# Row gathers ahead of a rarely taken branch, index products later, and row sums on another engine, in a kernel of attention and two mixtures of experts

## The chip, the cores and the metric

One core of one Trainium2 chip runs the whole kernel. The metric is the device time of one execution in microseconds (us). TensorE multiplies matrices, VectorE and ScalarE work on rows, GpSimd does so too and issues the gathers and scatters (indirect DMAs), and SP issues most plain loads. Each engine works through its own queue in order. In the profile they are PE (PEld for its weight loads), DVE, ACT, POOL and SP; a name with a q is the engine's sequencer or DMA queue.

## The reference

Attention over 8 heads (4 local, 4 strided), then two mixtures of experts (MoE), each row a token:

```python
x = attn(q, k, v)                                   # 1152 tokens x 512
logits = x @ w_gate + modality_bias[modality_id]    # MoE 1: 8 experts, each token goes to one
e_idx = argmax(logits, axis=1)
for e in range(8):
    out[e_idx == e] = gate * (relu(x[e_idx == e] @ w1[e]) @ w2[e])
for e in range(4):                                  # MoE 2: every token through all four
    y += p[:, e:e+1] * (relu(out @ w1b[e]) @ w2b[e])
```

## The kernel before

The work comes in four stretches. Attention and the router fill some 77 us. MoE 1 follows until about 205 us: the tokens of each expert are gathered by index into tiles of 128 rows. The fullest expert's first tile is done apart (`fill`). Two blocks of up to 464 tokens (`k` = 0 and 1, four tiles each, `NBT`) belong to the two fullest experts, a ninth tile (`S_ONE`) stands alone, and two small tiles (`NSM`, `sg`) hold up to 32 tokens of the experts with few. What doesn't fit goes through the body of `overflow` (L1515), which lies behind a chain of branches on the count `ntl_i` and isn't taken for these inputs. MoE 2 takes the rest of the time in units of hidden columns. A product in full float32 precision is made of three matmuls on high and low halves (`split`: ScalarE writes the high half, VectorE the low).

The schedule is written by hand. A loop over `n` runs layer 1 of block `k`, hidden chunk `fb` (`l1`, L1574), and two steps behind it layer 2 (`l2`, L1591). After each of them stands a `tick(k, fb, 0)` or `tick(k, fb, 1)` (L1761), which splits one more block of weights (`W.ahead`) and does what the table `todo` (L1741) has for that place. In this text (0,5,1) means the tick after layer 2 in step `fb` = 5 of block 0. The queues then follow the order in which the instructions are written.

Around the change:

- `slots_of` (L1056) computes from the router the list of token indices (`main.idx`) in small VectorE steps, given out by `steps`, and ends with matmuls that sum over tokens (L1152, L1153).
- `overflow` reads the count on every engine (L1516) and branches (L1521). Its body has a pool `op` with weight tiles `raw2_0..3`, rows `g` and `y`, and hidden tiles.
- `routed` (L1726) stands at (0,3,1): first `overflow`, then the pool `mp` on the memory that `op` gave back, with the split rows `xbh`, `xbl` of block 2 and its gathered tiles `gb`. Eight gathers on GpSimd fill them: four of rows (`xe`, L1622) and four of gates and other small values (`xx`, L738).
- `small_tiles` (L1632) loads the small tiles' weights in SP's queue and gathers `sg`; its matmuls are spread over the ticks from (0,6,0) on.
- `x_split(X[1], i, ...)` at (0,5,1) to (0,7,0) transposes a gathered tile into the PSUM bank `PA[0]` (L1171) and splits it (L1166, L1167) into `xbh` and `xbl`.
- `x2_load` (L1294) reads finished rows of MoE 1 back for MoE 2 from (1,2,0) on; `x2_prep` (L1321) transposes such a tile, takes four sums (L1311 to L1314) and four differences (L1319) on GpSimd, from (1,3,0) on.
- The tail (L1816 to L1844) weaves the ninth tile with the first unit of MoE 2; `PC.put(n)` splits `n` pieces of MoE 2's weights. A unit's fifth step ends with an addition on VectorE (L1448) that reads the PSUM bank which its sixth step goes on writing.

Block 2 in this text is the loop's second block, `k` = 1.

Of the kernel before, what the change touches and what calls it, by code (L numbers as in the profile page):

```python
# [20 lines left out]
P = 128  # L21
# [123 lines left out]
def fused_kernel(  # L145
# [1154 lines left out]
    def x2_sums(j, tt):  # L1300
# [10 lines left out]
        nc.gpsimd.tensor_tensor(t1, b12, b11, op=ALU.subtract)  # L1311
        nc.gpsimd.tensor_tensor(t2, b22, t1, op=ALU.subtract)
        nc.gpsimd.tensor_tensor(t4, b21, t2, op=ALU.subtract)
        nc.gpsimd.tensor_tensor(t3, b22, b12, op=ALU.subtract)  # L1314
        return b11, b21, b22

    def x2_split(h, l, src):
        nc.scalar.copy(h, src)
        nc.gpsimd.tensor_tensor(l, src, h.bitcast(F32), op=ALU.subtract)  # L1319

    def x2_prep(j):  # L1321

        cols = slice(HP * j, HP * (j + 1))
        t4 = ye0[:, :DM].rearrange("p (q c t) -> p q c t", q=4, c=2)
        b = x2_sums(j, [t4[:, i] for i in range(4)])
        gx.pop(j)
        for q, src in zip((QB11, QB21, QB22), b):
            x2_split(xh2[:, q, :, cols], xl2[:, q, :, cols], src)
        yield
        x2_split(xh2[:, QT1:, :, cols], xl2[:, QT1:, :, cols], t4)  # L1330

    def x2_late(j):
# [5 lines left out]
        b = x2_sums(j, tt)  # L1338
        gx.pop(j)
        for q, src in zip((QB11, QB21, QB22), b):  # L1340
            x2_split(*(x[:, :, cols] for x in XP[1][q]), src)
        yield
        for q, src in zip((QT1, QT2, QT3, QT4), tt):
            x2_split(*(x[:, :, cols] for x in XP[1][q]), src)
# [166 lines left out]
    with ExitStack() as mctx:  # L1511
# [3 lines left out]
        def overflow():  # L1515
# [3 lines left out]
            with tc.tile_pool(reuse_waits="tile", name="op", bufs=1) as op:  # L1519
                raws2 = [op.tile([P, 1024], F32, name=f"raw2_{i}") for i in range(KC)]  # L1520
# [111 lines left out]
        def small_tiles():  # L1632
# [14 lines left out]
            def fetch(n):  # L1647
                slot = [idxs[:, n : n + 1]]
                g = gathered(slot, mp, "sg", NSM)
                with_all(g, slot)  # L1650
                return g[0]

            for _ in ring:
                load()
            gs = [fetch(n) for n in range(NSM)]
# [58 lines left out]
        mp = None  # L1714
# [11 lines left out]
        def routed():  # L1726
            nonlocal small, mp
            overflow()
            mp = mctx.enter_context(tc.tile_pool(reuse_waits="tile", name="mp", bufs=1))
            X[1] = [mp.tile([P, KC, NBW], F32R, name=n) for n in ("xbh", "xbl")]  # L1730
            slots = [at(NBT + i) for i in range(NBT)]
            G[1] = gathered(slots, mp, "gb", NBT)
            with_all(G[1], slots)
            small = small_tiles()

        def fetch_one():
            G[2] = gathered([at(S_ONE)], gp, "g", None)
            with_all(G[2], [at(S_ONE)])
# [3 lines left out]
            (0, 0, 0): lambda: (steps(3), with_all(gA, [idx4[:, i : i + 1] for i in range(NBT)])),  # L1742
            (0, 1, 0): lambda: steps(2),
            (0, 2, 0): lambda: steps(2),
            (0, 2, 1): lambda: steps(1),
            (0, 3, 0): lambda: [0 for _ in rest],
            (0, 3, 1): routed,
            (0, 4, 0): copies,
            (0, 5, 0): lambda: next(small),
            (1, 2, 0): lambda: [x2_load(j) for j in range(CHT[0])],  # L1750
            (1, 2, 1): fetch_one,
# [3 lines left out]
        todo[1, 6, 1] = lambda: (split_one(), next(prep[3], None))  # L1755
        for j in range(CHT[0]):
            prep[j] = x2_prep(j)
            todo[1, 3 + j, 0] = lambda j=j: next(prep[j])
            todo.setdefault((1, 3 + j, 1), lambda j=j: next(prep[j], None))

        def tick(k, fb, n):  # L1761
# [6 lines left out]
            if (k, fb) >= (0, 6):  # L1768
                next(small, None)

        LAG = 2
        for n in range(2 * FC):
# [6 lines left out]
        bh, bl = (mp.tile([P, KC, NBW], F32, name=n).rearrange("p c n -> p (c n)") for n in ("xbh", "xbl"))  # L1779
# [52 lines left out]
        one_l2(0)  # L1832
        next(unit)
        next(unit)
        one_l2(1)
        PC.put(2)
        next(unit)
        next(unit)
# [209 lines left out]
```

## Time and profile before

| | us |
|---|---|
| median of 3 runs (lowest, highest) | 611.41 (610.82, 611.66) |
| the profiled execution | 608.61 |
| its span, first to last instruction | 606.8 |
| TensorE busy | 573.6 |
| VectorE busy | 355.3 |
| ScalarE busy | 284.7 |
| GpSimd busy | 242.3 |

The profile is one execution, so sums are made against its own time, 608.61. TensorE is busy in nearly all of the span. What it doesn't do is to be looked for in single waits, and in the stretches in which its granted clock is under 1.00 (1.00 is 2.4 GHz, the lower level is 1.2).

### The profile page before, as it was taken

The numbers are of one execution on the slowest core, as the hardware profiler recorded it, in microseconds if no ns is written. First come the engines' busy times: TensorE is split into PE (matmuls) and PEld (weight loads), VectorE is DVE, ScalarE is ACT, GpSimd is POOL, SyncE is SP. The second block draws the span as 40 slices with busy tenths as digits, with TensorE's granted clock in tenths as the row PEclk, the third lists the DMA queues.
The fourth block names the chain that finished last, engine by engine and source line by source line (L and its number), as shares of the span: only waits on it lengthen the run. The fifth ranks groups of instructions, "written<-read, shape, count | busy, mean of one in ns | idle before, by whom it ended". The sixth has DMA issues, their size and how long they took to land.

```text
span 606.8 us, 10107 instructions
## 1 busy us (share of the span) xinstructions
PE 573.6 (95%) x3746; PEld 483.1 (80%) x3746; DVE 355.3 (59%) x735; ACT 284.7 (47%) x617; POOL 242.3 (40%) x348
## 2 busy tenths in 40 slices
PE   8987987699799989999999999999999999999994
PEld 4555665577578878989889888989989899888893
DVE  6775877432224556686786776655575566557531
ACT  5754343333344645556656555444444444444410
POOL 6524332603566552455756674253222232222212
PEclk9999999889899989999999999999999999999998
DMA  8958423948923343524232232322223312111002
GB/s 261 314 127 278 154 88 109 321 181 273 326 75 105 120 177 110 187 73 136 70 129 80 86 123 71 138 88 105 87 70 98 111 71 70 69 70 70 0 9 79
DMA packets 33660, 77.55 MB, mean 128 GB/s; under 512 B 5856, under 2 KB 11882, under 8 KB 33477
## 3 DMA queue, kind: packets, MB, share of 16 engines
q1 hardware_dynamic: 28581, 65.66, 32.3%
q0 software_dynamic: 4736, 10.99, 5.4%
q8 instruction: 31, 0.51, 0.3%
q10 hardware_dynamic: 288, 0.19, 0.1%
q14 instruction: 24, 0.20, 0.1%
HBM read 73.46 MB, written 7.55 MB: 134 GB/s over the span
## 4 chain that ended last, share of the span: by engine, by line
PE 70%; issue 6%; DMA 3%; POOL 2%; DVE 1%; POOLq 0%; ACT 0%; DVEq 0%; ACTq 0%
PE ps_b L1436 10%; PE ps_b L1438 10%; PE ps_b L1437 10%; PE ps_b L1870 7%; PE ps_b L1869 7%; PE ps_b L1872 7%; PE ps_a L1870 4%; PE ps_a L1869 4%; PE ps_a L1872 4%; DMA g<-xc 1%; DMA sg<-xx,idxs 1%; PE ps_b L1600 1%; PE ps_b L1601 1%; PE ps_b L1602 1%; PE ps_a L1171 1%
## 5 line engine op out<-in xcount | busy, mean ns | idle before, releaser
L1358 DVE TENSOR_TENSOR wl<-stage,wh 128x512 fp32r<-128x512 f32 (+1 forms) x160 | 124.5, 780 | 58.7 <-ACT wh L1357 58.2
L1378 POOL TENSOR_TENSOR stage<-stage 128x256 f32<-128x256 f32 x32 | 24.0, 749 | 204.9 <-DVE wl L1358 204.9
L1357 ACT CAST wh<-stage 128x512 fp32r<-128x512 f32 (+1 forms) x160 | 102.8, 664 | 3.9 <-POOL mark L746 3.8
L1436 PE MATMUL ps_b<-x,wh 128*128 128x320 f32 x224 | 69.7, 311 | 0.2 <-DVE xl L1456 0.2
L1437 PE MATMUL ps_b<-x,wh 128*128 128x320 f32 x224 | 69.2, 309 | 0.0
L1438 PE MATMUL ps_b<-x,wl 128*128 128x320 f32 x224 | 69.0, 308 | 0.0
L1448 DVE TENSOR_TENSOR m2t<-ps_b,stage 128x320 f32<-128x320 f32 (+1 forms) x93 | 42.2, 453 | 41.0 <-PE ps_b L1438 39.9
L1436 PE MATMUL ps_b<-xh,wh 128*128 128x256 f32 x224 | 64.0, 286 | 2.2 <-DVE xbl L1448 2.2
L1438 PE MATMUL ps_b<-xh,wl 128*128 128x256 f32 x224 | 63.2, 282 | 0.0
L1437 PE MATMUL ps_b<-xl,wh 128*128 128x256 f32 x224 | 63.2, 282 | 0.0
L1436 PEld LDWEIGHTS ps_b<-xh,wh 128*128 128x128 f32 x224 | 42.5, 190 | 7.7 <-DVE xbl L1448 2.4
L1436 PEld LDWEIGHTS ps_b<-x,wh 128*128 128x128 f32 x224 | 42.0, 187 | 5.5 <-DVE xl L1456 0.4
L1437 PEld LDWEIGHTS ps_b<-xl,wh 128*128 128x128 f32 x224 | 42.5, 190 | 4.4
L1437 PEld LDWEIGHTS ps_b<-x,wh 128*128 128x128 f32 x224 | 42.1, 188 | 4.5
L1438 PEld LDWEIGHTS ps_b<-xh,wl 128*128 128x128 f32 x224 | 42.6, 190 | 0.0
L1438 PEld LDWEIGHTS ps_b<-x,wl 128*128 128x128 f32 x224 | 42.1, 188 | 0.0
L1451 ACT ACTIVATE hh2b<-m2t 128x256 fp32r<-128x256 f32 (+1 forms) x45 | 20.0, 444 | 43.3 <-DVE m2t L1448 40.8
L1167 DVE TENSOR_TENSOR wl<-stage,wh 128x1024 fp32r<-128x1024 f32 x24 | 30.6, 1280 | 15.5 <-ACT wh L1166 15.5
L1451 ACT ACTIVATE hh2a<-m2t 128x256 fp32r<-128x256 f32 (+1 forms) x42 | 18.7, 445 | 44.5 <-DVE m2t L1448 44.5
L1870 PE MATMUL ps_b<-wl,hh2b 128*128 128x512 f32 x90 | 35.7, 396 | 0.0
L1870 PE MATMUL ps_b<-wl,hh2a 128*128 128x512 f32 x90 | 35.5, 395 | 0.0
L1869 PE MATMUL ps_b<-wh,hh2a 128*128 128x512 f32 x90 | 35.5, 395 | 0.0
(398 smaller groups left out, 1411.0 us busy)
## 6 DMA issues: line engine op xcount, KB each, us to landing
stage<-in_w1b_dram SPq DMA_DIRECT2D x32, 512.0 KB
stage<-in_w2b_dram SPq DMA_DIRECT2D x32, 512.0 KB
stage<-in_w1a_dram SPq DMA_DIRECT2D x24, 512.0 KB
stage<-in_w2a_dram SPq DMA_DIRECT2D x24, 512.0 KB
g<-xc SPq DMA_DIRECT2D x5, 260.0 KB
vl<-in_vlo_dram SPq DMA_DIRECT2D x2, 520.0 KB
g<-xc POOLq DMA_DIRECT2D x4, 260.0 KB, 8.2
xe<-rw POOLq DMA_DIRECT2D x7, 128.0 KB, 5.4
```

What stands on the lines that cost most here:

```text
L1167: nc.vector.tensor_tensor(dst_l, src, dst_h.bitcast(F32), op=ALU.subtract)
L1357: return (lambda: nc.scalar.copy(h[:, s], src[:, s])), (lambda: nc.vector.tensor_tensor(l[:, s], src[:, s], h[:, s].bitcast(F32), op=ALU.s ...
L1358: lambda: nc.vector.tensor_tensor(l[:, s], src[:, s], h[:, s].bitcast(F32), op=ALU.subtract)
L1378: nc.gpsimd.tensor_tensor(a22, a22, a21, op=ALU.add)
L1436: nc.tensor.matmul(ph, wh[:, kc], xh, start=first and kc == 0, stop=False, skip_group_check=True)
L1437: nc.tensor.matmul(ph, wh[:, kc], xl, start=False, stop=False, skip_group_check=True)
L1438: nc.tensor.matmul(ph, wl[:, kc], xh, start=False, stop=kc == 1, skip_group_check=True)
L1448: nc.vector.tensor_tensor(t, a, b, op=ALU.add)
L1451: nc.scalar.activation(h, a, AF.Relu)
L1869: nc.tensor.matmul(po, hh, wh, start=(fb == 0 and fh == 1), stop=False, skip_group_check=part)
L1870: nc.tensor.matmul(po, hh, wl, start=False, stop=False, skip_group_check=part)
L1872: nc.tensor.matmul(po, hl, wh, start=False, stop=last, skip_group_check=part)
```

## The change

The gathers of block 2 and of the small tiles, and that of the ninth tile's rows, are written ahead of `overflow`. All their `xx` gathers follow right before it, at (0,5,0). The branch's body uses `raws[KC:]`, the weight buffers of block 1's second layer, for `raw2`. Block 2's tiles come from the pool `gp`, `sg` and the ninth tile from `mp`, which is opened ahead of the branch; only `xbh` and `xbl` lie on what `op` gives back (pool `mx`). The index products (the rest of `slots_of`) move from (0,3,0) to (0,4,0). One index step and one weight split are done ahead of the loop. The small tiles' first matmuls start a tick later. `x2_load` moves to (1,1,1), `x2_prep` to (1,4,0) to (1,5,1), one whole tile per tick, with its sums and differences on VectorE (`nc.vector`). One of the two pieces of `PC.put(2)` in the tail goes ahead by a few steps, one behind the next unit step.

```diff
--- before.py
+++ after.py
@@ -1297,7 +1297,7 @@
         eng.dma_start(out=g, in_=xc[P * j : P * (j + 1), :])
         gx[j] = g
 
-    def x2_sums(j, tt):
+    def x2_sums(j, tt, eng):
 
         g = gx[j]
         nc.gpsimd.tensor_copy(ext2[:, j], g[:, DM:])
@@ -1308,26 +1308,26 @@
         b = xr.rearrange("p (k c h t) -> p k c h t", k=2, c=2, h=2)
         b12, b21, b22, b11 = b[:, 0, :, 1], b[:, 1, :, 0], b[:, 1, :, 1], b[:, 0, :, 0]
         t1, t2, t3, t4 = tt
-        nc.gpsimd.tensor_tensor(t1, b12, b11, op=ALU.subtract)
-        nc.gpsimd.tensor_tensor(t2, b22, t1, op=ALU.subtract)
-        nc.gpsimd.tensor_tensor(t4, b21, t2, op=ALU.subtract)
-        nc.gpsimd.tensor_tensor(t3, b22, b12, op=ALU.subtract)
+        eng.tensor_tensor(t1, b12, b11, op=ALU.subtract)
+        eng.tensor_tensor(t2, b22, t1, op=ALU.subtract)
+        eng.tensor_tensor(t4, b21, t2, op=ALU.subtract)
+        eng.tensor_tensor(t3, b22, b12, op=ALU.subtract)
         return b11, b21, b22
 
-    def x2_split(h, l, src):
+    def x2_split(h, l, src, eng):
         nc.scalar.copy(h, src)
-        nc.gpsimd.tensor_tensor(l, src, h.bitcast(F32), op=ALU.subtract)
+        eng.tensor_tensor(l, src, h.bitcast(F32), op=ALU.subtract)
 
     def x2_prep(j):
 
         cols = slice(HP * j, HP * (j + 1))
         t4 = ye0[:, :DM].rearrange("p (q c t) -> p q c t", q=4, c=2)
-        b = x2_sums(j, [t4[:, i] for i in range(4)])
+        b = x2_sums(j, [t4[:, i] for i in range(4)], nc.vector)
         gx.pop(j)
         for q, src in zip((QB11, QB21, QB22), b):
-            x2_split(xh2[:, q, :, cols], xl2[:, q, :, cols], src)
-        yield
-        x2_split(xh2[:, QT1:, :, cols], xl2[:, QT1:, :, cols], t4)
+            x2_split(xh2[:, q, :, cols], xl2[:, q, :, cols], src, nc.vector)
+        yield
+        x2_split(xh2[:, QT1:, :, cols], xl2[:, QT1:, :, cols], t4, nc.vector)
 
     def x2_late(j):
 
@@ -1335,13 +1335,13 @@
         cols = slice(HP * i, HP * (i + 1))
         t4 = raws[6][:, :DM].rearrange("p (q c t) -> p q c t", q=4, c=2)
         tt = [t4[:, k] for k in range(4)]
-        b = x2_sums(j, tt)
+        b = x2_sums(j, tt, nc.gpsimd)
         gx.pop(j)
         for q, src in zip((QB11, QB21, QB22), b):
-            x2_split(*(x[:, :, cols] for x in XP[1][q]), src)
+            x2_split(*(x[:, :, cols] for x in XP[1][q]), src, nc.gpsimd)
         yield
         for q, src in zip((QT1, QT2, QT3, QT4), tt):
-            x2_split(*(x[:, :, cols] for x in XP[1][q]), src)
+            x2_split(*(x[:, :, cols] for x in XP[1][q]), src, nc.gpsimd)
 
     XP = {}
     RING2 = 8
@@ -1517,7 +1517,8 @@
                 ntl_i[0:1, 0:1], min_val=0, max_val=NSX, skip_runtime_bounds_check_because="bounded by the token count"
             )
             with tc.tile_pool(reuse_waits="tile", name="op", bufs=1) as op:
-                raws2 = [op.tile([P, 1024], F32, name=f"raw2_{i}") for i in range(KC)]
+                raws2 = raws[KC:]
+                assert W.ns >= 2 * KC
                 with ExitStack() as more:
                     more.enter_context(tc.If(ntl > S_OVF))
                     for t in range(S_OVF, NSX):
@@ -1644,15 +1645,9 @@
                     load_block(raw, todo.pop(0))
                     loaded.append(raw)
 
-            def fetch(n):
-                slot = [idxs[:, n : n + 1]]
-                g = gathered(slot, mp, "sg", NSM)
-                with_all(g, slot)
-                return g[0]
-
             for _ in ring:
                 load()
-            gs = [fetch(n) for n in range(NSM)]
+            gs = G["s"]
             yield
             used = 0
             bank = PA[1]
@@ -1711,7 +1706,8 @@
                 yield
 
         prep = {}
-        mp = None
+        mp = mctx.enter_context(tc.tile_pool(reuse_waits="tile", name="mp", bufs=1))
+        mx = None
 
         def copies():
             pr = PA[1][:, 64 : 64 + NSM]
@@ -1723,40 +1719,51 @@
             for _ in range(n):
                 next(rest)
 
-        def routed():
-            nonlocal small, mp
+        slotsB = []
+        slots_s = [idxs[:, n : n + 1] for n in range(NSM)]
+
+        def second_rows():
+            for _ in rest:
+                pass
+            slotsB.extend(at(NBT + i) for i in range(NBT))
+            G[1] = gathered(slotsB, gp, "g", None)
+
+        def small_rows():
+            copies()
+            G["s"] = gathered(slots_s, mp, "sg", NSM)
+            G[2] = gathered([at(S_ONE)], mp, "sone", 1)
+
+        def gates():
+            with_all(G[1], slotsB)
+            with_all(G["s"], slots_s)
+            with_all(G[2], [at(S_ONE)])
             overflow()
-            mp = mctx.enter_context(tc.tile_pool(reuse_waits="tile", name="mp", bufs=1))
-            X[1] = [mp.tile([P, KC, NBW], F32R, name=n) for n in ("xbh", "xbl")]
-            slots = [at(NBT + i) for i in range(NBT)]
-            G[1] = gathered(slots, mp, "gb", NBT)
-            with_all(G[1], slots)
+            mx = mctx.enter_context(tc.tile_pool(reuse_waits="tile", name="mx", bufs=1))
+            X[1] = [mx.tile([P, KC, NBW], F32R, name=n) for n in ("xbh", "xbl")]
+            return mx
+
+        def branch():
+            nonlocal small, mx
+            mx = gates()
             small = small_tiles()
-
-        def fetch_one():
-            G[2] = gathered([at(S_ONE)], gp, "g", None)
-            with_all(G[2], [at(S_ONE)])
+            next(small)
 
         small = None
         todo = {
-            (0, 0, 0): lambda: (steps(3), with_all(gA, [idx4[:, i : i + 1] for i in range(NBT)])),
+            (0, 0, 0): lambda: (steps(2), with_all(gA, [idx4[:, i : i + 1] for i in range(NBT)])),
             (0, 1, 0): lambda: steps(2),
-            (0, 2, 0): lambda: steps(2),
-            (0, 2, 1): lambda: steps(1),
-            (0, 3, 0): lambda: [0 for _ in rest],
-            (0, 3, 1): routed,
-            (0, 4, 0): copies,
-            (0, 5, 0): lambda: next(small),
-            (1, 2, 0): lambda: [x2_load(j) for j in range(CHT[0])],
-            (1, 2, 1): fetch_one,
+            (0, 2, 0): lambda: steps(3),
+            (0, 4, 0): second_rows,
+            (0, 4, 1): small_rows,
+            (0, 5, 0): branch,
+            (1, 1, 1): lambda: [x2_load(j) for j in range(CHT[0])],
         }
         for i in range(NBT):
             todo[0, 5 + (i + 1) // 2, (i + 1) % 2] = lambda i=i: x_split(X[1], i, G[1][i], PA[0])
-        todo[1, 6, 1] = lambda: (split_one(), next(prep[3], None))
+        todo[1, 6, 1] = split_one
         for j in range(CHT[0]):
             prep[j] = x2_prep(j)
-            todo[1, 3 + j, 0] = lambda j=j: next(prep[j])
-            todo.setdefault((1, 3 + j, 1), lambda j=j: next(prep[j], None))
+            todo[1, 3 + (j + 2) // 2, j % 2] = lambda j=j: [0 for _ in prep[j]]
 
         def tick(k, fb, n):
             early_ = (k, fb) < (0, 4)
@@ -1765,10 +1772,12 @@
             todo.get((k, fb, n), lambda: None)()
             if not early_:
                 W.ahead(RING, 1)
-            if (k, fb) >= (0, 6):
+            if (k, fb, n) >= (0, 6, 1):
                 next(small, None)
 
         LAG = 2
+        steps(1)
+        W.ahead(RING, 1)
         for n in range(2 * FC):
             k, fb = divmod(n, FC)
             l1(k, fb)
@@ -1776,7 +1785,7 @@
             if n >= LAG:
                 l2(*divmod(n - LAG, FC))
                 tick(k, fb, 1)
-        bh, bl = (mp.tile([P, KC, NBW], F32, name=n).rearrange("p c n -> p (c n)") for n in ("xbh", "xbl"))
+        bh, bl = (mx.tile([P, KC, NBW], F32, name=n).rearrange("p c n -> p (c n)") for n in ("xbh", "xbl"))
         first = {k: bl[:, 256 * i : 256 * (i + 1)] for i, k in enumerate("tabd")}
         sh = bh[:, :FF]
         parts = [hidden_parts() for _ in range(2)]
@@ -1830,11 +1839,12 @@
         one_htr(1)
         next(unit)
         one_l2(0)
+        PC.put(1)
         next(unit)
         next(unit)
         one_l2(1)
-        PC.put(2)
         next(unit)
+        PC.put(1)
         next(unit)
         one_l2(2)
         next(unit)
```

## Rows read from the trace of the kernel before

**Rows 1.** Waits of TensorE: line, releaser, us in all, times, longest

```profile
PE ps_a L1171 <- DMA sg<-xe,idxs: 4.9, 1, 4.9
...
PE ps_a L1171 <- DMA g<-xc: 3.6, 1, 3.6
...
PE ps_b L1436 <- DVE xbl L1448: 2.2, 1, 2.2
...
PE ps_a L1153 <- DVE bos L1147: 1.9, 1, 1.9
...
PE ps_b L1601 <- DVE wl L1167: 1.8, 1, 1.8
...
PE ps_b L1581 <- PEq L1521: 1.4, 1, 1.4
```

**Rows 2.** Stretches: us, busy PE, PEld, DVE, ACT, POOL, then PEclk, DMA, GB/s

```profile
75.00:100.00 25.00, 20.03 (x99) 15.08 (x98) 19.70 (x57) 9.56 (x13) 4.97 (x5) 1.00 0.30 98
...
119.30:124.80 5.50, 5.49 (x16) 4.27 (x16) 0.00 (x0) 0.59 (x1) 0.00 (x0) 0.51 0.59 225
...
162.50:166.00 3.50, 3.46 (x12) 3.03 (x13) 0.02 (x1) 2.28 (x6) 1.67 (x5) 0.56 0.98 393
...
215.40:220.40 5.00, 4.97 (x21) 4.36 (x22) 2.47 (x6) 2.52 (x6) 1.73 (x4) 0.66 0.16 61
...
166.00:194.00 28.00, 28.00 (x191) 22.37 (x191) 10.45 (x10) 13.70 (x28) 20.99 (x34) 1.00 0.25 81
...
221.00:600.00 379.00, 376.90 (x2206) 338.61 (x2205) 237.66 (x405) 184.01 (x407) 145.45 (x199) 1.00 0.26 91
```

**Rows 3.** L1516, L1521: xcount, ns min/median/max, first to last start us

```profile
L1516 POOLq TENSOR_LOAD <-ntl_i x1: 485/485/485, 80.4 to 80.4; - x1
...
L1521 POOLq EVENT_SEMAPHORE  x4: 17/43/43, 86.5 to 87.1; - x4
...
L1521 POOLq INC_SWDGE_SEM  x1: 796/796/796, 87.2 to 87.2; - x1
...
L1521 SPq EVENT_SEMAPHORE  x9: 17/17/17, 101.0 to 101.6; - x9
```

**Rows 4.** Timeline of GpSimd: start us, us, line, operation [idle <- releaser]

```profile
84.08 0.94 POOL L738 DMA_INDIRECT g<-xx,idx  x1 [0.30 <-issue]
...
101.92 0.94 POOL L1622 DMA_INDIRECT gb<-xe,idx  x1 [16.90 <-SPq L1521]
...
118.07 0.12 POOL L746 MEMSET mark<- 128x1 f32 x1
```

**Rows 5.** Timeline of SP, its loads around the branch

```profile
96.57 0.33 SPq L197 DMA_DIRECT2D stage<-in_w1a_dram  x1
...
107.25 5.09 SPq L197 DMA_DIRECT2D stage<-in_w1a_dram  x5
```

**Rows 6.** Tile gb, its eight gathers, issue to landing

```profile
DMA to landing us min/median/max: 2.8/6.0/7.8
```

**Rows 7.** Timeline of TensorE: transposes and the layer behind

```profile
119.31 1.11 PE L1171 MATMUL ps_a<-mk,sg 128*128 128x128 f32 x4 [4.89 <-DMA sg<-xe,idxs]
...
120.08 0.77 PE L1600 MATMUL ps_b<-wh,hh 128*128 128x512 f32 x1
...
171.19 0.60 PE L1171 MATMUL ps_a<-mk,g 128*128 128x128 f32 x4
```

**Rows 8.** Timeline of VectorE: a relu's low half, a tile's low half

```profile
102.73 0.64 DVE L1589 SCALAR_TENSOR_TENSOR hl<-ps_b,hh 128x464 fp32r<-128x464 f32 x1 [3.79 <-ACT hh L1588]
...
112.10 0.69 DVE L1167 TENSOR_TENSOR xbl<-ps_a,xbh 128x512 fp32r<-128x512 f32 x1 [1.08 <-ACT xbh L1166]
```

**Rows 9.** Timeline of GpSimd: the loads for MoE 2

```profile
155.94 2.25 POOL L1297 DMA_DIRECT2D g<-xc  x4 [3.34 <-DMA xc<-g,dest]
```

**Rows 10.** Timeline of VectorE: weight pieces, then the addition

```profile
212.35 2.69 DVE L1358 TENSOR_TENSOR wl<-stage,wh 128x768 fp32r<-128x768 f32 x3 [0.32 <-ACT wh L1357]
...
214.97 0.41 DVE L1448 TENSOR_TENSOR xbl<-ps_b,xbl 128x256 f32<-128x256 f32 x1
```

## The prediction

> **What bounds the kernel now.** I read the waits of TensorE first, because the chain that ends last runs through it. Only six waits over 1.3 us lie between 85 and 216 us [rows 1]. Then the table by stretch: from 221 us on, TensorE is busy 376.9 of 379 us at a granted clock of 1.00 [rows 2]. So the second mixture of experts (MoE 2) is a solid block, and what the stages before it win or lose arrives at the end one to one. The same table shows a second price of some waits: after the waits of 4.9, 3.6 and 2.2 us the granted clock was 0.51, 0.56 and 0.66 for 5.5, 3.5 and 5.0 us, so TensorE ran at the lower level (1.2 GHz) for part of each; after those of 1.4 to 1.9 us it stayed 1.00. Length times missing clock gives 2.7, 1.5 and 1.7 us.
>
> The profiled execution took 608.6 us (span 606.8), 2.8 us less than the median of 611.4. I sum against 608.6 and carry the difference of 2.8 over.
>
> **Parts that cost nothing or are covered.** One index step and one weight split move ahead of the loop. VectorE and ScalarE have only that to do before the first relu, and the third block's split then comes one layer-1 step (2.6 us) earlier, so the 1.8 us wait at L1601 goes. The index products move from (0,3,0) to (0,4,0), by when the counts (L1147) are done: the 1.9 us wait goes. The two gathers of the ninth tile (sone) join GpSimd's early burst and leave its queue at 158 us. Neither 1.8 nor 1.9 reaches the end by itself, since what follows is tied to GpSimd, below.
>
> **The branch: where the front gain goes.** Before, the gathers stood behind the branch. GpSimd itself had passed it: four events at 86.5 to 87.1 and one of 0.8 us at 87.2 [rows 3]. But the first gather waited 16.9 us, until 101.9, for SP's events at 101.0 to 101.6 [rows 3, 4], because its tile lies on memory that the branch's body uses. SP's events came 4.4 us after its last load was issued (96.57) [rows 5]; GpSimd's came 2.4 us after its last gather was issued (84.08) [rows 4]. I read both the same way: an engine reports the branch passed only when everything that it had issued before has landed, and whoever reuses the body's memory waits for that report.
>
> The change takes the gathers out of that wait, but puts fourteen of them (four rows of block 2, two small, one ninth, then seven of `xx`) ahead of the branch on GpSimd. The memory that is now laid over the body's g, y and he is `xbh`, first written by ScalarE in `x_split` at (0,5,1). So ScalarE waits for GpSimd's report, T:
> - The index is there when layer 1 of (0,4) is done. VectorE took up its low half at 102.73 [rows 8]; less 1.8 + 1.9 + 1.4 of waits and about 0.5 of products that lay ahead of it, that is 97.1. Add 0.6 (the low half), 0.2 (the index copy) and 0.3 (issue): the first gather starts at 98.2.
> - The fourteenth starts 13 paces later. One gather is 0.94 + 0.30 = 1.24 in a quiet stretch; the twelve of before took 101.92 to 118.07, 1.35 each [rows 4]. I take 1.3: 16.9.
> - It lands 2.8 to 7.8 us after issue [rows 6]; I take the middle, 5.3, since SP's loads are in flight. The report adds 0.9 (as 87.2 to 88.0).
> - T = 98.2 + 16.9 + 5.3 + 0.9 = 121.3; ends 118.0 (1.24, 2.8) and 124.4 (1.35, 7.8).
>
> Behind ScalarE's waiting instruction stand the next weight split and the relu of (0,6). TensorE, having split the first tile at about 107 and done layer 1 of (0,6), needs bank PA[0] for the second `x_split` at about 110 and waits there. After T come ScalarE 0.59 (its one copy of a tile, 128x512, in the stretch from 119.3 [rows 2]), VectorE 0.69 [rows 8], some 0.2 of handing over, and 0.77 for four transposes at the low clock (119.31 to 120.08) [rows 7]: layer 2 of (0,4) starts at T + 2.2, and 0.4 for the small tile's transposes is still owed. Before, it started at 120.08 with those done [rows 7]. The balance is T + 2.6 - 120.1 = T - 117.5 = **+3.8 us**, ends +0.5 and +6.9. The waits of 4.9, 1.9 and 1.8 are gone and one of some 12 stands for them; the low clock after it I take as before. The small tile's own gather, issued by 105, is no longer late. The branch's 1.4 on TensorE moves to (0,5,0) and hides under that wait; SP passes when its last load has landed, around 107, as it started the small weights at 107.25 before [rows 5].
>
> **Loading for MoE 2: -5.1 us.** The loads `g<-xc` were issued at 155.94, after 3.34 us for the last scatter's landing [rows 9], and TensorE waited 3.6 us for the first. Issuing them at (1,1,1) doesn't change that: they wait for the same scatter, except that the small tile's scatter now stands behind them. It must then wait for them to land, and GpSimd with it, but nobody needs that row soon. What helps is that the first transposes move from after layer 1 of (1,3) to after that of (1,4). The second tile's transposes stood there at 171.19 [rows 7]; less 162.5, where the first began, and less 1.5 for the low clock, that is some 7 us later. So 7 against 3.6: the wait and its low clock go, 3.6 + 1.5 = 5.1. If landing is late again, the clock's part may stay: 3.6 at the least.
>
> The sums now run on VectorE: per tile seven operations of 128x128 and one of 128x512. The trace has no such operation on VectorE. By its 128x512 split (0.69 [rows 8]) a quarter is 0.17 at least, and 0.41 (its 128x256 addition, [rows 10]) at most; I take 0.3, so 2.8 us a tile, 11 in all. VectorE was busy 10.5 of 28 us there [rows 2] and two steps lie between a relu and its use, so I cost it at nothing; at 0.41 it would be some 14, and about 1 us might show.
>
> **The hand-over to MoE 2: -3.0 us.** The 2.2 us wait at L1436 is for VectorE's addition at 214.97, which stood behind three weight pieces begun at 212.35 [rows 10]; two of them came from `PC.put(2)` right before that unit step. With one put moved ahead and one behind, I expect the pieces done by about 213.5 and the addition at once behind: a wait of some 0.9 is left, since the next product writes the bank that the addition reads. That is 1.3, and 1.7 of low clock, as waits under 2 us left the clock at 1.00. Ends: 0 (the pieces' load lands no earlier) and 3.9.
>
> **Sum.** 608.6 + 3.8 - 5.1 - 3.0 = 604.3 profiled, 607.1 as a median. All ends together: -8.5 and +3.3, so 602.9 to 614.7.
>
> **Rivals.**
> *The branch doesn't hold ScalarE.* If GpSimd's delay were only the jump, its report would come early: it read the branch's value at 80.4, while its gathers ran on until 85 [rows 3, 4], so its sequencer runs ahead. With the small index at about 101 and ten issues of 0.3 it is through at 104; 80.4 to 88.0 is 7.6 more: T = 111.6, -5.9 instead of +3.8: 597.4. With no wait on memory at all, 1.8 + 1.9 + 4.9 + 2.7 = 11.3 come off: 592.0. Against it: the 16.9 us wait, and the two reports that follow landings. The Trainium skill ("Runtime: NRT & Kernel Launch", Instruction fetch mechanics) says that a taken branch whose target isn't in the fetched window stalls for a fetch of it. By that rule the gaps after the branch would be fetches and the first of these two times would follow; the trace has such gaps but, as they differ between the engines and end with landings, doesn't bear it out alone. Chance 0.12 together.
>
> *The loads stay late.* If the burst and the small weights crowd the transfers so that `g<-xc` lands 3 us later against the work, or the put order wins nothing, some 3 of the 8.1 are lost: 610 to 611, within 0.2%. Chance 0.14.
>
> *Slower: GpSimd reports so late that the wait outgrows the rest.* The break-even is T = 117.5 + 8.1 = 125.6. SP's five loads, issued over 5.09 us from 107.25 [rows 5], fall just ahead of the last gathers. If those then need 12 us instead of at most 7.8, at 1.35 apiece, T = 98.2 + 17.5 + 12 + 0.9 = 128.6 and the time is 611.4 + 11.1 - 8.1 = 614.4. For it: landing already reached 7.8 under such load; against: those loads should be nearly through by 115. Chance 0.09.
>
> **How the numbers follow.** Forecast 0.65, rivals 0.12, 0.14, 0.09. The range of 602 to 613 takes in nearly all of the forecast, the second rival and the mild end of the third; it leaves out the first and the bad ends, under 2 in 10. About 0.2% (1.2 us) is what a measurement can tell from no change. Faster by more: 0.59 of the forecast, the first rival, and a little of the second, 0.73. Within: 0.15. Slower: the third and the forecast's worst end, 0.12.
>
> **What would show it.** In the changed profile: waits at L1601, L1153 and for `sg` gone; gathers on GpSimd from about 98 without a break; its branch events near 121; TensorE waiting some 12 us around 110 to 122 at L1171 for `gb`'s successor, with ScalarE's `xbh` behind GpSimd; no wait for `g<-xc`; under 1.5 us at L1436, the clock at 1.00 behind it; MoE 2 as long as before. It is wrong if `xbh` follows its transposes at once (much faster), or if the events come after 125 (no gain).

## The result and the profile after

| | time, us | ratio to before |
|---|---|---|
| before | 611.6 median (608.9 to 615.3) | |
| changed | 606.0 median (602.5 to 610.2) | 0.991, 95% interval 0.989 to 0.993 |
| profiled execution of the changed kernel | 607.0, span 605.3 | |

The change gains 5.6 us by the medians; 607.1 was predicted. The two profiled executions differ by 1.6 us only: single executions of either kernel scatter by some 3 us to both sides, and the one of before was 3 us under its median. So stretches of the two traces show what moved, and the medians what it is worth.

The waits of TensorE over 1.3 us between 90 and 225 us (tile, line, who released it, total, times, longest) answer to [rows 1]. Six waits have become three, and one is longer than all of the others together:

```profile
PE ps_a L1171 <- DVE xbl L1167: 11.6, 1, 11.6
PE ps_b L1601 <- PEq L1522: 2.5, 1, 2.5
PE ps_b L1436 <- DVE xbl L1448: 1.9, 1, 1.9
```

The waits for `sg`, `g<-xc`, `bos` and `wl` are gone. The chain that ended last in 95 to 130 us (start, us, what) tells where the 11.6 us come from, and the branch's line gives each engine's branch events (count, shortest/median/longest in ns, first and last start):

```profile
115.39 6.70 DMA sone<-xx,idx
...
122.48 0.59 ACT xbh L1166
...
123.09 0.70 DVE xbl L1167
...
123.84 1.12 PE ps_a L1171 x4
```

```profile
L1522 SPq EVENT_SEMAPHORE  x9: 2/17/704, 107.5 to 109.4; - x9
L1522 POOLq EVENT_SEMAPHORE  x4: 17/43/9302, 111.5 to 121.0; - x4
L1522 PEldq COMPARE_BRANCH  x1: 4652/4652/4652, 99.9 to 99.9; - x1
...
L1522 ACTq COMPARE_BRANCH  x1: 50/50/50, 102.8 to 102.8; - x1
L1522 DVEq COMPARE_BRANCH  x1: 72/72/72, 103.5 to 103.5; - x1
...
L1522 ACTq EVENT_SEMAPHORE  x1: 17/17/17, 108.1 to 108.1; - x1
L1522 POOLq COMPARE_BRANCH  x1: 53/53/53, 111.0 to 111.0; - x1
L1522 POOLq INC_SWDGE_SEM  x1: 1076/1076/1076, 121.1 to 121.1; - x1
```

GpSimd reaches the branch at 111.0, but one of its four events lasts 9.3 us, until the last of its fourteen gathers has landed. That one was issued at 115.39, the last packet of GpSimd's queue ended at 120.30 by the trace's transfer records, and the event at 120.88; the 6.70 us of the chain have the rest of the report (to 122.1) in them. ScalarE's first `xbh` follows at once, then VectorE, then TensorE. Layer 2 of (0,4) starts at 124.61; before, it was 120.08 [rows 7]. On GpSimd's timeline (start, us, operation, idle before it and who ended it) the gathers run from 97.74 without a break, where before the first came at 101.92 [rows 4]:

```profile
97.74 0.95 POOL L1623 DMA_INDIRECT g<-xe,idx  x1 [12.46 <-DVE cum L1157]
...
115.39 0.94 POOL L738 DMA_INDIRECT sone<-xx,idx  x1 [0.30 <-issue]
```

The table by stretch (as [rows 2]: us, busy PE, PEld, DVE, ACT, POOL, clock, DMA share, GB/s) has the low clock behind the long wait as before, 0.50 over 5.5 us against 0.51, but 1.00 where it had been 0.56 and 0.66. From 221 us on it shows the same solid block as before:

```profile
123.80:129.30 5.50, 5.46 (x15) 4.32 (x16) 3.60 (x4) 2.20 (x4) 0.00 (x0) 0.50 0.35 118
...
162.50:166.00 3.50, 3.50 (x28) 2.28 (x27) 1.87 (x2) 1.77 (x3) 1.19 (x3) 1.00 1.00 296
...
214.50:220.00 5.50, 5.18 (x31) 4.63 (x32) 5.09 (x9) 3.64 (x7) 1.62 (x3) 1.00 0.31 102
221.00:600.00 379.00, 375.27 (x2193) 336.53 (x2191) 236.94 (x403) 182.22 (x404) 144.96 (x199) 1.00 0.26 90
```

### The profile page after: what moved, and what is told of

The parts are those of the page before. It is cut to its first block, busy times and chain, and to the rows that moved or that the text cites. A ratio compares the mean times of both kernels' runs of the same rounds, so it can differ in the third digit from the quotient of the medians.

```text
span 605.3 us, 10092 instructions
## 1 busy us (share of the span) xinstructions
PE 573.7 (95%) x3746; PEld 482.7 (80%) x3746; DVE 363.7 (60%) x767; ACT 284.7 (47%) x617; POOL 221.6 (37%) x316
## 4 chain that ended last, share of the span: by engine, by line
PE 76%; DMA 2%; DVE 1%; issue 1%; ACT 0%; POOL 0%; POOLq 0%; ACTq 0%
PE ps_b L1436 10%; PE ps_b L1437 10%; PE ps_b L1438 10%; PE ps_b L1880 7%; PE ps_b L1879 7%; PE ps_b L1882 7%; PE ps_a L1880 4%; PE ps_a L1879 4%; PE ps_a L1882 4%; PE ps_b L1601 2%; PE ps_b L1602 2%; PE ps_b L1603 2%; PE ps_b L1582 1%; PE ps_b L1584 1%; PE ps_b L1583 1%; PE ps_a L1171 1%
## 5 line engine op out<-in xcount | busy, mean ns | idle before, releaser
L1436 PE MATMUL ps_b<-x,wh 128*128 128x320 f32 x224 | 69.7, 311 | 0.2 <-DVE xl L1456 0.2
L1448 DVE TENSOR_TENSOR m2t<-ps_b,stage 128x320 f32<-128x320 f32 (+1 forms) x93 | 42.2, 454 | 40.4 <-PE ps_b L1438 37.8
L1436 PE MATMUL ps_b<-xh,wh 128*128 128x256 f32 x224 | 63.9, 285 | 1.9 <-DVE xbl L1448 1.9
L1436 PEld LDWEIGHTS ps_b<-xh,wh 128*128 128x128 f32 x224 | 42.2, 188 | 8.1 <-DVE xbl L1448 2.1
L1436 PEld LDWEIGHTS ps_b<-x,wh 128*128 128x128 f32 x224 | 42.0, 187 | 5.4 <-DVE xl L1456 0.4
L1167 DVE TENSOR_TENSOR wl<-stage,wh 128x1024 fp32r<-128x1024 f32 x24 | 29.2, 1222 | 14.6 <-ACT wh L1166 8.5
```

What stands on the lines that cost most here:

```text
L1167: nc.vector.tensor_tensor(dst_l, src, dst_h.bitcast(F32), op=ALU.subtract)
L1436: nc.tensor.matmul(ph, wh[:, kc], xh, start=first and kc == 0, stop=False, skip_group_check=True)
L1448: nc.vector.tensor_tensor(t, a, b, op=ALU.add)
```

## Experiments

Each was timed against the kernel before on the same chip; "gain" is against the changed kernel's 606.0. The kernel before had medians from 610.1 to 611.6 in these rounds, so where two medians of different rounds differ by little, the ratios decide.

| kernel | median, us | ratio to before, 95% interval |
|---|---|---|
| front_alone | 616.3 | 1.009 (1.006 to 1.012) |
| no_x2 | 613.6 | 1.004 (1.001 to 1.006) |
| before_put | 608.7 | 0.998 (0.996 to 1.001) |
| no_put | 607.3 | 0.994 (0.991 to 0.998) |
| sums_on_gpsimd | 607.0 | 0.993 (0.990 to 0.996) |
| before_x2 | 604.5 | 0.991 (0.989 to 0.994) |
| own_rows | 599.6 | 0.981 (0.977 to 0.985) |
| gates_behind | 597.1 | 0.977 (0.972 to 0.982) |
| early_branch | 593.4 | 0.974 (0.970 to 0.978) |
| own_rows_four_behind | 592.8 | 0.972 (0.969 to 0.974) |
| own_rows_gates_behind | 592.3 | 0.967 (0.964 to 0.971) |
| no_branch | 590.9 | 0.969 (0.964 to 0.974) |

### The parts, one by one

**front_alone**: x2 and `PC.put` as before, only the changes around the branch kept.

```diff
-        b = x2_sums(j, [t4[:, i] for i in range(4)], nc.vector)
+        b = x2_sums(j, [t4[:, i] for i in range(4)], nc.gpsimd)
...
-            (1, 1, 1): lambda: [x2_load(j) for j in range(CHT[0])],
+            (1, 2, 0): lambda: [x2_load(j) for j in range(CHT[0])],
...
-            todo[1, 3 + (j + 2) // 2, j % 2] = lambda j=j: [0 for _ in prep[j]]
+            todo[1, 3 + j, 0] = lambda j=j: next(prep[j])
+            todo.setdefault((1, 3 + j, 1), lambda j=j: next(prep[j], None))
...
         one_l2(0)
-        PC.put(1)
         next(unit)
         next(unit)
         one_l2(1)
+        PC.put(2)
         next(unit)
-        PC.put(1)
```

> The changed kernel with the loading for MoE 2 put back (loads at (1,2,0), sums on GpSimd at the old steps) and both of the PC.put back in one place: only the changes around the branch are left. By the prediction's sum the front alone costs +3.8 (ends +0.5 and +6.9) against the kernel before: 612.1 to 618.5 beside a median of 611.6, middle 615.4, with waits of some 12 us at L1171, 3.6 us for the loads g<-xc and 2.2 us at L1436. Rival (the medians of the two kernels differ by 5.6 us although the profiled pair differs by 1.6, so the front was worth nothing or a gain): 609 to 612.

It is 5.2 us slower than the kernel before (611.1 on that chip), by the ratio 5.4 with an interval of 3.7 to 7.1. The predicted +3.8 and its ends hold; the rival, that the front is worth nothing, falls. The waits are those expected, with 4.7 us for `g<-xc` in place of 3.6 and 13.7 at L1171, since GpSimd's report ended 2.0 us later in this execution (124.1) than in the changed kernel's:

```profile
PE ps_a L1171 <- DVE xbl L1167: 13.7, 1, 13.7
PE ps_a L1171 <- DMA g<-xc: 4.7, 1, 4.7
PE ps_b L1601 <- PEq L1522: 2.6, 1, 2.6
PE ps_b L1436 <- DVE xbl L1448: 2.2, 1, 2.2
```

**no_x2**: the changed kernel with the x2 part of that diff alone.

> The changed kernel with the loading for MoE 2 as before: the loads g<-xc at (1,2,0), the row sums and splits on GpSimd at the old steps. With the changed kernel's front alone the wait for these loads was 4.7 us and the granted clock behind it 0.94 over 28 us (1.7 us), so the later loads should cost 4.7 + 1.7 = 6.4 us here: 612.4. By the prediction's own term (5.1): 611.1. Rival (alone in the kernel before the move was worth 5 to 6 us, but here the small tile's scatter stands behind the loads): 607 to 609.

613.6: the loading for MoE 2 is worth 7.6 us in the changed kernel. The wait for `g<-xc` is 4.7 us, until 166.75, and the clock then stays low: 0.50 until 170 and 0.76 over the next 4 us, which loses 1.6 and 1.0 us. That makes 7.3 by the profile, where I had put 3.6 + 1.5:

```profile
166.75 1.12 PE L1171 MATMUL ps_a<-mk,g 128*128 128x128 f32 x4 [4.74 <-DMA g<-xc]
```

```profile
166.00:170.00 4.00, 3.25 (x21) 0.50 0.24 96
170.00:174.00 4.00, 4.00 (x16) 0.76 0.28 99
```

**before_x2**: the same part alone in the kernel before.

> The kernel before with the loading for MoE 2 alone changed: the loads g<-xc at (1,1,1), the row sums and splits on VectorE, at the changed kernel's steps. By the prediction -5.1 us (at the least -3.6), so 606 to 607.5 beside 611.3; the wait of 3.6 us for g<-xc and the low clock behind it go, and VectorE's sums show nowhere on TensorE. Rival (the gain needs the front's other order, or the sums delay the relu): 609 to 612.

604.5 beside 610.8: 6.3 us by the medians, 5.3 by the ratio (3.5 to 7.0). Here the wait that goes is the one of 3.6 us [rows 1], so the term of 5.1 is confirmed at its own place; in the changed kernel it grew because the wait it takes away had grown. The earlier place of the loads isn't what helps: GpSimd still issues them only after 3.46 us of waiting for the last scatter, where it was 3.34 [rows 9], as the prediction had it:

```profile
160.93 2.25 POOL L1297 DMA_DIRECT2D g<-xc  x4 [3.46 <-DMA xc<-g,dest]
```

**sums_on_gpsimd**: loads and steps as changed, `nc.vector` back to `nc.gpsimd` in `x2_prep`.

> The changed kernel with the loads and steps as changed, but the row sums and splits of x2 on GpSimd. On GpSimd a tile took 7.1 us in the kernel before (162.55 to 169.71), while the changed kernel's tiles come 4.4 us apart (169.34, 173.77, 177.95, 182.37), so GpSimd would finish the fourth at about 198 instead of 187, just as MoE 2 begins, and with the weight sums of MoE 2 behind it: +1 to +4 us, 607 to 610. Rival (the engine doesn't matter, the steps alone give the gain): 606. Rival (the sums hold the bank or the one buffer that the next tile needs): waits of 2 us and more at L1171 between 170 and 185, over 610.

607.0 beside the changed kernel's 606.0, no difference that can be told. My expectation took a tile on GpSimd at 7.1 us, but that had its waits for ScalarE in it; here the same operation of two tiles starts at 174.55 and at 179.11, 4.6 us apart, hardly more than the transposes, and GpSimd is through at 193.5, while its next work for MoE 2 starts at 201.80. So the gain doesn't come from the engine, nor from the earlier loads (before_x2). The later steps are left as its source; no run has them alone.

```profile
174.55 0.46 POOL L1313 TENSOR_TENSOR ye<-g,ye 128x128 f32<-128x128 f32 x1
...
179.11 0.46 POOL L1313 TENSOR_TENSOR ye<-g,ye 128x128 f32<-128x128 f32 x1
...
192.23 1.30 POOL L1319 TENSOR_TENSOR xl<-ye,xh 128x512 fp32r<-128x512 f32 x1
201.80 0.74 POOL L1378 TENSOR_TENSOR stage<-stage 128x256 f32<-128x256 f32 x1 [8.27 <-DVE wl L1358]
```

**before_put** and **no_put**: `PC.put(2)` split alone in the kernel before, and joined again in the changed one.

```diff
         one_l2(0)
+        PC.put(1)
         next(unit)
         next(unit)
         one_l2(1)
-        PC.put(2)
         next(unit)
+        PC.put(1)
```

> The kernel before with PC.put(2) alone split in two. By the prediction -3.0 us (ends 0 and -3.9): 608.3 beside 611.3, a wait of about 0.9 us at L1436 and no low clock behind it. Rival (the wait stays near 2 us since the piece's load is what ends last): 611.

> The changed kernel with the two pieces of weights for MoE 2 in one PC.put(2) again, behind one_l2(1). By the prediction the split of the two is worth 3.0 us (ends 0 and 3.9): 609.0 beside the changed kernel's 606.0, a wait of about 2.2 us at L1436 near 214 us and a granted clock of about 0.66 for 5 us behind it. Rival (the profiled pair shows a wait of 1.9 instead of 2.2, so the order of pieces is worth 0.3 us and at most the low clock's 1.7): 606 to 608.

Between front_alone and no_x2 the split is worth 2.6 us (by the ratios 3.2), in the kernel before 2.2 (by the ratio 1.2, -0.4 to 2.8, so no gain is shown there), in the changed one 1.3 (by the ratios 1.9). The intervals reach some 2 us to either side. 3.0 lies in two of them and just outside that of before_put, and the likeliest size is some 2 us. The wait at L1436 in before_put is 1.1, near the predicted 0.9. VectorE's timeline shows why. In no_put the addition (L1448) at 216.74 stands behind three pieces that run for 2.69 us, as in [rows 10]; in before_put it stands behind one, at 213.77:

```profile
214.13 2.69 DVE L1358 TENSOR_TENSOR wl<-stage,wh 128x768 fp32r<-128x768 f32 x3 [0.32 <-ACT wh L1357]
216.74 0.41 DVE L1448 TENSOR_TENSOR xbl<-ps_b,xbl 128x256 f32<-128x256 f32 x1
```

```profile
212.68 1.17 DVE L1358 TENSOR_TENSOR wl<-stage,wh 128x512 fp32r<-128x512 f32 x1 [0.20 <-ACT wh L1357]
213.77 0.41 DVE L1448 TENSOR_TENSOR xbl<-ps_b,xbl 128x256 f32<-128x256 f32 x1
```

The clock's share was less sure than I took it. The wait was 2.2 us in four executions. Behind it the granted clock was 0.66 in the kernel before [rows 2], and 0.50 and then 0.84 over 6 us in front_alone (224 to 230 us), which loses 1.6 us; but it stayed at 1.00 in no_put and before_x2 (216 to 222 us).

### The branch

**gates_behind**: the seven gathers of gate rows move behind the branch.

```diff
+            overflow()
             with_all(G[1], slotsB)
             with_all(G["s"], slots_s)
             with_all(G[2], [at(S_ONE)])
-            overflow()
```

> The changed kernel with one thing moved: the seven small gathers of gate rows (from xx) stand behind the branch instead of ahead of it; the seven gathers of token rows (from xe) stay ahead. Theory (ScalarE's first write of xbh waits for GpSimd's report of the branch, which comes when all of its earlier gathers have landed): seven paces of 1.3 us less ahead of the branch bring the report from 122.2 to about 113, the wait at L1171 falls from 11.6 to about 2.5 us, and the time from 606.0 to about 597. Rival A (TensorE and ScalarE wait for the rows of block 2 themselves to land, behind which the branch stands by accident): the rows are issued as before, so the wait stays at 11 to 12 us and the time at 606. Rival B (the time lost is that of the branch itself, a jump with a fixed price): the report moves, but the wait stays over 8 us, 603 to 606.

597.1, as the theory gave. GpSimd has reported at 114.3 (113.4 and 0.94), 14.9 us after its first gather at 99.47; in the changed kernel it was 24.4 us (97.74 to 122.1). That is 9.5 less, for 9.1 expected, and the wait of 11.6 us is 2.1. Rivals A and B fall. The trace's transfer records bear the theory out wherever the kernel has a branch. In all thirteen executions GpSimd's report (`INC_SWDGE_SEM`) starts 0.4 to 0.8 us after the last packet of its gathers, though from 6 to 13 us after its jump.

```profile
L1522 SPq EVENT_SEMAPHORE  x9: 17/17/17, 109.4 to 110.1; - x9
L1522 POOLq EVENT_SEMAPHORE  x4: 17/43/43, 113.1 to 113.3; - x4
...
L1522 POOLq COMPARE_BRANCH  x1: 53/53/53, 102.2 to 102.2; - x1
...
L1522 POOLq INC_SWDGE_SEM  x1: 936/936/936, 113.4 to 113.4; - x1
```

```profile
PE ps_b L1601 <- PEq L1522: 2.4, 1, 2.4
PE ps_a L1171 <- DVE xbl L1167: 2.1, 1, 2.1
```

**own_rows**: the body's two row tiles get memory that nothing else uses, so `xbh` and `xbl` lie over `he` and `hte` alone.

```diff
+        og, oy = (mp.tile([P, XW], F32, name=n, bufs=1) for n in ("og", "oy"))
...
-                            g = op.tile([P, XW], F32, name="g")
+                            g = og
...
-                            lambda: op.tile([P, XW], F32, name="y"),
+                            lambda: oy,
```

> The changed kernel with the branch body's two row tiles (g, y, which only GpSimd and the body fill) on memory of their own, so that xbh and xbl lie over the body's he and hte alone, which GpSimd never touches. All gathers stay ahead of the branch. Theory (it is the shared memory that ties ScalarE to GpSimd's report): the report still comes near 122, but ScalarE's first xbh copy follows its transposes at about 108 to 109; the wait of 11.6 us at L1171 and the low clock behind it go, up to 14 us, and I expect 592 to 597 us. Rival A (the rows themselves land late): the wait stays, 606. Rival B (a branch stops every engine until the last one is through it, whatever memory it uses): the wait stays, 606. Rival C (the front isn't worth what its wait shows, since the weight loads become the next thing late): 600 to 603, with new waits for wl or wh between 125 and 165.

599.6: 6.4 us gained, less than the 9 to 14 of the theory. GpSimd's report comes as late as ever (an event of 12.3 us, ended at 121.6), but `xbh` is written at 107.37, so the memory was the tie. Rivals A and B fall as stated. But a wait of 4.3 us is left at L1171, which is not for weights (rival C): ScalarE's relu of (0,6) starts at 113.11 and its next `xbh` at 115.97, although the records of the products and transposes that they read end at 109.83 and 110.27; the profile knows no releaser ("remote"). ScalarE isn't alone in being late: one of SP's nine events behind the branch takes 694 ns, in gates_behind none over 17.

```profile
L1522 SPq EVENT_SEMAPHORE  x9: 2/13/694, 105.3 to 107.3; - x9
L1522 POOLq EVENT_SEMAPHORE  x4: 17/43/12276, 109.2 to 121.6; - x4
```

```profile
107.37 0.59 ACT L1166 CAST xbh<-ps_a 128x512 fp32r<-128x512 f32 x1 [0.56 <-PE ps_a L1171]
...
113.11 0.56 ACT L1589 ACTIVATE hh<-ps_b 128x464 fp32r<-128x464 f32 x1 [4.20 <-remote]
115.97 0.59 ACT L1166 CAST xbh<-ps_a 128x512 fp32r<-128x512 f32 x1 [2.31 <-remote]
```

```profile
117.34 0.90 PE L1171 MATMUL ps_a<-mk,g 128*128 128x128 f32 x3 [4.28 <-DVE xbl L1167]
```

**own_rows_gates_behind**: both edits. **own_rows_four_behind**: own_rows with `with_all(G[1], slotsB)` alone behind the branch.

> Both of the earlier changes at once: the body's row tiles on memory of their own, and the gathers of gate rows behind the branch. Alone they gave 9.0 and 6.4 us below the changed kernel's 606.0. Theory (both take away the same wait of ScalarE for GpSimd's report): they don't add, 596 to 600. Rival (two separate causes, the shared memory and the transfers of the gate rows): they add, 590 to 592.

> As own_rows (599.6), but the four gate-row gathers of block 2 stand behind the branch and three (two small tiles, the ninth tile) stay ahead; with all seven behind it was 592.3. What is open: why TensorE still waited 4.3 us in own_rows, with ScalarE's relu of (0,6) at 113.1 though its products ended at 109.8. Theory (gate rows that are in flight while the engines come back from the branch at 106 to 110 hold them up, in proportion): GpSimd issues its last of ten by about 110 instead of 114, a wait of 0 to 2 us at L1171, 593 to 596. Rival (any gate gather ahead of the branch, since GpSimd's report then stands open while the others run on): the wait stays near 4 us, 598 to 600.

The first says that I was wrong: 592.3, the gains nearly add (8.9 + 6.4 = 15.3; measured 13.7; by the ratios 14.8 and 14.4). So gate gathers ahead of the branch cost time in a second way, beside the report. The second run says where: with the four of block 2 behind the branch and three still ahead it is 592.8, the wait at L1171 is gone, and the relu of (0,6) starts 0.6 us after its products:

```profile
PE ps_b L1601 <- PEq L1522: 2.1, 1, 2.1
PE ps_b L1436 <- ACT stage L1469: 1.3, 1, 1.3
```

```profile
113.78 0.56 ACT L1589 ACTIVATE hh<-ps_b 128x464 fp32r<-128x464 f32 x1 [1.46 <-PE ps_a L1171]
```

The rival (any gate gather ahead holds) falls. The theory's time is right within 0.2 us, but not its picture: the three still left GpSimd between 108.7 and 112.9, inside the stretch in which I had wanted the transfers empty. What the four gathers hold up is open: in own_rows the release of the relu came 3.3 us after its products, and no run shows through what. The gathers alone don't do it. In early_branch, below, all seven run beside the same products (105.7 to 115.7), in no_branch beside those of the next step (106.8 to 116.9), and no such wait follows. What these two lack is the branch right behind the gathers.

**no_branch**: the call of `overflow()` left out.

> The changed kernel without the branch for overflowing tiles at all (the tiles that it would compute are left out; these inputs have none). It prices everything that hangs on the branch. Theory: as with the body's row tiles on their own memory, and TensorE's 2.5 us at the branch and its low clock go too, SP's and VectorE's stops (5.8 us on VectorE) as well: the front runs without a wait over 2 us, 590 to 595 us. Rival (what is late next is the weights or the rows, not the branch): waits of the same length under other names, over 600 us.

590.9, with no wait over 2 us. It is 15.1 us under the changed kernel, of which the two edits above recover 13.7. What the branch costs by itself at this place can't be told from nothing: own_rows_gates_behind lies 1.4 us above by the medians and 0.9 below by the ratios, although TensorE stands still for 2.1 to 2.8 us at the branch in the kernels that have it here.

**early_branch**: the branch and the index products at their old places, the body's weights in buffers of its own, and all gathers behind the branch.

```diff
-                raws2 = raws[KC:]
+                raws2 = [op.tile([P, 1024], F32, name=f"raw2_{i}") for i in range(KC)]
...
         def second_rows():
-            for _ in rest:
-                pass
+            nonlocal mp, mx
+            overflow()
+            mp = mx = mctx.enter_context(tc.tile_pool(reuse_waits="tile", name="mp", bufs=1))
+            X[1] = [mx.tile([P, KC, NBW], F32R, name=n) for n in ("xbh", "xbl")]
...
         def gates():
...
-            overflow()
...
-            (0, 4, 0): second_rows,
-            (0, 4, 1): small_rows,
+            (0, 3, 0): lambda: [0 for _ in rest],
+            (0, 3, 1): second_rows,
+            (0, 4, 0): small_rows,
```

> The changed kernel with the branch back at its place of before, (0,3,1), with buffers of its own for the body's weights as before, and with all fourteen gathers behind it; block 2's rows still go into freed buffers of the pool gp (no memory of the body), the small tiles' rows into the memory behind xbl. xbh and xbl lie over the body's weight buffers, so they wait for SyncE's report alone, which came at 101 in the kernel before. Theory: what the changed kernel lost at the branch was the memory tie and the branch's own stop at a place where GpSimd and SyncE have much in flight; here neither lies on the path: no wait over 2 us at L1171, 1.4 to 2 us of TensorE at the branch and 1.9 us for bos, and 591 to 597 us. Rival A (a branch costs its 5 us jump on every engine wherever it stands, and own_rows has all that moving the memory can give): 598 to 602. Rival B (gathers behind the branch wait again for SyncE's report, as before): first gather at 101 or later, 603 to 610.

593.4, where 591 to 597 was expected; both rivals fall. The first gather starts at 95.09, 2.4 us ahead of SyncE's report, since its tile shares no memory with the body. GpSimd, with only the first block's gathers ahead of the branch, has reported by 87.2.

```profile
95.09 0.94 POOL L1622 DMA_INDIRECT g<-xe,idx  x1 [10.61 <-DVE cum L1157]
```

```profile
L1521 SPq EVENT_SEMAPHORE  x9: 17/17/17, 97.5 to 98.0; - x9
...
L1521 POOLq COMPARE_BRANCH  x1: 53/53/53, 80.7 to 80.7; - x1
L1521 POOLq INC_SWDGE_SEM  x1: 796/796/796, 86.4 to 86.4; - x1
```

So two versions that keep the branch beat both kernels: own_rows_gates_behind at 592.3 and early_branch at 593.4, 13.7 and 12.6 us under the changed one (by the ratios 14.4 and 10.2).

## Why the prediction was right, point by point

- **T.** Predicted: first gather 98.2, pace 1.3, landing 5.3, report 0.9, T = 121.3. Measured: 97.74, (115.39 - 97.74) / 13 = 1.36, 6.70 by the chain with the report in it, T = 122.1. The mechanism is shown by gates_behind (seven paces off, -8.9 us) and by own_rows (other memory, and `xbh` no longer waits). It is shown for GpSimd alone. I had read SP's report the same way, but there a fixed price of the jump fits better: in the four executions with the branch at (0,3,1) SP's first event came 3.6 to 3.7 us after its jump, and 0.6 to 1.2 us after its last load had landed. The prediction's T doesn't use SP's report.
- **The front.** +3.8 predicted; 4.5 between the two traces (124.61 to 120.08); +5.2 as front_alone. Two things were low. One is T: over the five executions with this front GpSimd's report ended 22.5 to 26.5 us after its first gather, 24.4 in the changed kernel's, where I had 23.1. The other is the wait for `g<-xc`, which grew to 4.7 in this front and which I had counted at 3.6. By the timelines it grew because a small tile's scatter, ahead of block 1's four in the kernel before (146.17), now stands between them and the loads (155.97 in no_x2); no run tests that alone.
- **The branch on TensorE.** I had its 1.4 us move and hide. It did hide, but it became 2.5 us, and TensorE ran at the lower clock behind it (0.56 between 107 and 109 us). Here the wait for T covers it. What it would cost in the versions without the tie isn't shown (no_branch).
- **Loading for MoE 2.** -5.1 predicted. In the kernel before 5.3 to 6.3; in the changed one 7.6. Mis-sized was the wait that it removes, 4.7 instead of 3.6, and the clock behind it, 2.6 instead of 1.5. VectorE's sums cost 0.28 to 0.29 us each, 0.3 predicted, and no wait; but the move to VectorE gains nothing either.
- **Hand-over.** -3.0 predicted, 1.2 to 3.2 measured. The residual wait, 0.9 predicted, was 0.5 to 1.2 in eight of the ten executions with the pieces apart, but 1.8 in sums_on_gpsimd and 1.9 in the changed kernel, over the 1.5 that I had set as a sign. In the changed kernel the piece ahead of the addition waits 1.12 for ScalarE, which waits for the piece's load. The clock of 1.7 that I counted isn't always lost.
- **The sum** was right to 1.1 us, in part by luck. By front_alone, no_x2 and the changed kernel in turn, the front is +5.2, the put -2.6 and the loading -7.6: -5.0 together, for -4.3 predicted. The front came out 1.4 worse, the put 0.4 worse, the loading 2.5 better. In the front and in the loading 1.1 of that is the same longer wait for `g<-xc`, which the one adds and the other takes away again. Nothing in the prediction makes the rest cancel.
- **The rivals.** "The branch doesn't hold ScalarE" was priced at 597.4 and 592.0. As a forecast it failed. That 592.3 is near its second price is luck: with the tie alone gone (own_rows) it is 599.6, and the rest comes from moving gathers, of which the rival says nothing. The Trainium skill ("Runtime: NRT & Kernel Launch", Instruction fetch mechanics) has a taken branch stall when its target isn't in the fetched window. On four engines the trace fits that: TensorE's jump took 4.65 us, ScalarE, SyncE and VectorE did nothing for 5.3 to 5.8 us behind theirs, and the queues for instructions moved eight blocks of 8 or 16 KB between 98 and 123 us. On GpSimd only 0.5 us lie between the jump (111.0) and the first event. Its 9.3 us are a wait for landings, and moving seven gathers shortened them, so the rule doesn't give the time of this change.

## What to carry to other kernels

In this kernel GpSimd reported a branch that wasn't taken only when the gathers that it had issued ahead of it had landed, and ScalarE, which writes memory that the branch's body uses, waited for that report. So look at what each engine has in flight where a branch stands, and at whose memory its body shares. Memory of its own for what GpSimd fills in the body (two tiles of 2 KB a partition) gave 6.4 us here, and seven small gathers moved behind the branch 8.9. When a step is moved away from a wait, price the wait that it will meet in the new order, not the one in the old trace.

## What the runs showed that I had not expected

- The jump of a branch that isn't taken held TensorE's queue for 3.4 to 5.0 us. In the kernels that have it at (0,5,0), 5.0 to 6.5 us passed until the next event of ScalarE and SyncE and the next operation of VectorE; in early_branch it was 2.7 us on ScalarE (90.7 to 93.4) and 3.7 on SyncE.
- With seven gate gathers ahead of the branch, a relu was released 3.3 us after its products had ended by their records; with three, 0.6 us. In the seven executions with gate gathers ahead of the branch one of SP's events behind it took 0.5 to 1.4 us, in the six others none over 17 ns; with three such gathers it was 0.7 us, though, and ScalarE wasn't late. Why is open.
- The same wait of 2.2 us at L1436 was followed by the lower clock in two executions and by 1.00 in two others.
